# A slot table for a chunked recurrence: decay work three chunks ahead, the inverse spread over more slots, lower quarters of two batches one chunk later

## The chip, the cores and the metric

The kernel runs on one core of a Trainium2 chip. The metric is the device time of one execution in microseconds (us). TensorE (PE), VectorE (DVE), ScalarE (ACT), GpSimd (POOL) and SyncE (SP) run side by side, each works through its own instructions in order, and they wait for each other and for DMA transfers through semaphores.

## The reference

A linear recurrence with a rank-one correction is followed by a gated MLP and a top-1 mixture of experts. There are 4 batches, 8 heads, 768 tokens and 40 dimensions a head; the MLP is 320 to 1536 and back, and the mixture has 8 experts of 320 x 1024.

```python
for t in range(S):                                    # S = 768
    y[:, :, t] = einsum('bhd,bhde->bhe', rt, state)
    Sa = einsum('bhde,bhe->bhd', state, at)
    state = state * wt[:, :, None, :] - einsum('bhd,bhe->bhde', Sa, bt)
    state = state + einsum('bhd,bhe->bhde', vt, kt)
x = y as (B*S, H*D)                                   # 3072 x 320
x = ((x @ w_a) * (x @ w_b)) @ w_out
logits = x @ w_gate; e = argmax(logits)
out = softmax(logits)[e] * (relu(x @ w1[e]) @ w2[e])
```

## The kernel before, in words

The 768 tokens are cut into 12 chunks of 64. Within a chunk the recurrence becomes matrix products: the decays `w` are scanned into products from both sides, `a`, `b` and `k` are scaled by them, a 128 x 64 block of scores is made for each head, and a unit lower triangular 64 x 64 matrix is inverted for each batch and head. The inverse is made of two 32 x 32 diagonal blocks, done on VectorE for all heads at once in 31 steps of a multiply and a subtract (62 instructions, `tinv`), and of a lower quarter that joins them, done on TensorE (`t21a`, `t21b`).

`phase1` runs 13 passes of 24 slots, c = 0 to 12. In pass c stand beside each other:
- `A.stage`: the recurrence of chunk c itself, its state and outputs.
- `t21a` and `t21b` of the four batches b of chunk c+1. `t21a` transposes the upper diagonal block on VectorE into `t11`, and TensorE's product `ta` reads `t11`.
- The preparation of chunk c+2. `load` brings the decays `w` and `bk` (b and k together). `spans` is the check that all decays lie in the range for which the fast path is meant: four ACT activations, of which only the accumulated sums are kept and whose output `span` is thrown away. `scans` is a clip of `w`, a scan from behind (`suf`), a copy and a reciprocal, and a scan from ahead (into `w`). `scale_bk` is four VectorE multiplies of `bk` with `suf`. `scale_a` loads `at`, scales it on GpSimd and spreads it into the block-diagonal `ablk` by three DMAs. `scores` is TensorE's s1p from `bk` and `ablk`, ACT's copy, a mask on GpSimd, and after every second batch two DMAs into `nd` in DRAM. `rows` are transposes of `bk` into `kb`. `relayout` is a set of DMAs from `w` into `gp`. `tinv` starts with three DMAs, `m` in two halves from `nd` and `xt` from a constant, and ends with four DMAs into `td` in DRAM and four back into `s1`.
- MoE-up of chunk c-1: 24 groups of eight matmuls into a PSUM buffer `pm`, one in a slot from slot 2 on. ACT copies one group's result to `ua`, VectorE multiplies it with the next group's into `uh`, a slot later, and `hT<-uh` is sent two slots after that. `pm` has three buffers.
- Conversion of weights, and in passes 2 to 9 one DMA `xs<-zt` each, which fills an eighth of a table in DRAM with zeros (slot 17).

All other PSUM tiles of these stages come from five buffers `pa`. After the passes come the down projection, the gating and the experts.

TensorE, VectorE, ACT and GpSimd run in the order in which the program is written: the tables `STEADY` and `FIRST` (the latter for pass 0) give the slot of each piece. In a slot, the tasks that were put off with `dv.later(k, f)` are mixed evenly among the steps of the inverse; `ot.later(k, f)` are run at the head of the slot k later. SP, which issues nearly all DMAs, has an order of its own that a scheduler makes from the dependences. The completion semaphores of SP's DMAs are eight in rotation, and a DMA waits for the one that stands eight places ahead of it.

In the print below, `i` is the slot, `c1` and `c2` are the chunks one and two ahead.

Of the kernel before, what the change touches and what calls it, by code (L numbers as in the profile page):

```python
# [8 lines left out]
F32 = mybir.dt.float32  # L9
# [4 lines left out]
AF = mybir.ActivationFunctionType  # L14
# [118 lines left out]
def phase1(tc, I, cst, drm, psA, psM, ident, hT, mk_ident, wo, xs, span, tiny, down):  # L133
# [23 lines left out]
    mk_ident()  # L157
    A.zero([A.rblk])
    A.setup()
    A.spans(1)  # L160
    A.scale_a(0, 0)
    A.scale_a(0, 1)
    run(A.scale_bk(0))
# [35 lines left out]
    A.spans(0, [t[:120, 0:L // 2].bitcast(F32) for t in sp])  # L199
    units, tinv = [], []  # L200
    for c in range(NCH + 1):
        T = dict(STEADY)
        if c == 0:
            T.update(FIRST)
        assert T["span"] <= T["scan"] <= T["bk"] and T["scan"] < min(T["sa"])
        c1, c2 = c + 1, c + 2
        if c >= 1:
            units += M.groups(c - 1)
        if 0 < c < NCH:
            A.begin(c)  # L210
        at = lambda k, i: [b for b in range(B) if T[k][b] == i]
        for i in range(24):
            run(ot.take())
            if c == NCH and down:
                if i == LAST["free"]:
                    mid.close()
                    down.begin()
                    M.spare = down.p2
                if i >= LAST["gate"]:
                    run(down.gate_steps(1))  # L220
                for j in range(3):
                    if i == LAST["load"][j]:
                        down.load(j)
                for j in range(2):
                    if i == LAST["w"][j]:
                        down.load_w(4 * j + 4)
                    if i == LAST["conv"][j]:
                        down.conv(j)
            M.early = M.early and i < FIRST["early"]
            if c < NCH:  # L230
                A.stage(c, i)
            if c1 < NCH:
                for pr in range(2):
                    if i == T["vload"][pr]:
# [41 lines left out]
            n = min(len(tinv), T["steps"]) if i >= T["tinv"] else 0  # L276
            mix(tinv[:n], dv.take() + more)
            tinv = tinv[n:]
            if i == 23 and c2 < NCH:
                A.relayout(c2)  # L280
                tinv = A.tinv(c2)
            dv.now += 1
            ot.now += 1
# [7 lines left out]
    if not down:  # L291
# [76 lines left out]
class Attention:  # L368
    def __init__(self, tc, I, ctx1, ctx2, cst, drm, ps, ident, dv, ot, span):
# [64 lines left out]
    def spans(self, c, room=None):  # L434
# [65 lines left out]
    def scores(self, c, b):  # L500
# [9 lines left out]
        if b % 2 == 0:  # L510
# [1179 lines left out]
```

## Time and profile before

| | us |
|---|---|
| three runs | 1395.9, 1395.37, 1392.11 |
| their median | 1395.37 |
| the profiled execution | 1392.37 |
| its span in the trace | 1390.6 |
| passes 1 to 9 (175.7 to 856.0) | 680.3 |
| TensorE busy in its span | 1223.3 (88%) |
| VectorE, ACT, GpSimd busy | 682.6, 525.4, 428.1 |

The profile is one execution, recorded on the chip. A busy TensorE is one that has a matmul under way; the granted clock (PEclk) says at which of its levels, as a share of full speed, it ran over a stretch. The idle time of an engine is put down to what it waited for last. SPq is the issue of DMAs on SP. Passes of the slot loop are told apart by the first matmul of slot 0, `px<-sgT,at`.

### The profile page before, as it was taken

To read this page: it belongs to the slowest core of one execution; us is meant where nothing else is said; L and a number is where in the kernel's file an instruction comes from. 1 tells how busy PE (TensorE), PEld (TensorE's weight loads), DVE (VectorE), ACT (ScalarE), POOL (GpSimd) and SP (SyncE) were. 2 spreads that over 40 slices of the span, in tenths; PEclk is the share of its full clock that TensorE was granted. 3 is DMA by queue.
4 is the path that set the end of the run, shared out by engine and by line. 5 is a ranking of instruction groups with operands and counts; after the bars stand their busy time and mean duration, and the time that the engine had idled before them with its cause. 6 is when DMAs were issued, how large, how long until landed. Compare 5 with 4: busy or idle time off the path is not lost.

```text
span 1390.6 us, 27472 instructions
## 1 busy us (share of the span) xinstructions
PE 1223.3 (88%) x10474; PEld 1150.1 (83%) x10474; DVE 682.6 (49%) x1867; ACT 525.4 (38%) x1301; POOL 428.1 (31%) x488
## 2 busy tenths in 40 slices
PE   2306898989898999989898999999999989999995
PEld 2306798888897988888897889999999988999995
DVE  7487454452838265463737273611345676322321
ACT  3535532324343333434342423332333344444541
POOL 5443521111222213221222121213011254766650
PEclk9555569969898797999898999999899999999998
DMA  7353343435557364845443432313545554635420
GB/s 186 97 150 88 89 107 78 113 82 133 117 137 143 93 151 105 170 104 142 102 121 84 121 78 83 83 49 104 170 128 175 178 181 144 199 125 147 147 75 15
DMA packets 252909, 166.63 MB, mean 120 GB/s; under 512 B 158675, under 2 KB 236196, under 8 KB 252770
## 3 DMA queue, kind: packets, MB, share of 16 engines
q1 hardware_dynamic: 238545, 141.17, 40.0%
q0 software_dynamic: 9808, 15.76, 3.8%
q10 hardware_dynamic: 4416, 7.87, 2.0%
q8 instruction: 85, 1.39, 0.4%
q14 instruction: 55, 0.44, 0.1%
HBM read 111.76 MB, written 44.60 MB: 112 GB/s over the span
## 4 chain that ended last, share of the span: by engine, by line
PE 57%; DVE 18%; DMA 9%; issue 3%; ACT 3%; POOL 1%; SPq 1%; POOLq 0%; ACTq 0%; DVEq 0%
PE pm L929 14%; PE py L1066 7%; PE u L1355 6%; PE dn L1375 6%; DVE tmp L577 4%; DVE xt L583 4%; PE pu L700 3%; PE px L681 3%; PE ta L617 2%; DMA m<-nd 2%; PE py L762 2%; PE px L678 2%; PE s1p L506 2%; PE p L740 2%; PE pp L722 2%
## 5 line engine op out<-in xcount | busy, mean ns | idle before, releaser
L941 DVE TENSOR_TENSOR uh<-pm,ua 128x256 f32<-128x256 f32 x144 | 60.9, 423 | 307.1 <-PE pm L929 229.1
L929 PE MATMUL pm<-xl,wh 128*128 128x256 f32 x576 | 149.8, 344 | 30.8 <-DVE uh L941 30.3
L747 POOL TENSOR_SCALAR_AFFINE_SELECT s<-s 64x512 f32<-64x512 f32 x96 | 74.2, 773 | 257.8 <-ACT s L745 254.7
L577 DVE TENSOR_TENSOR tmp<-m,xt 128x126 f32<-128x126 f32 (+22 forms) x372 | 115.9, 314 | 28.7 <-DMA m<-nd 13.7
L929 PEld LDWEIGHTS pm<-xl,wh 128*128 128x128 f32 x576 | 94.9, 206 | 38.3 <-DVE uh L941 33.2
L929 PE MATMUL pm<-xh,wl 128*128 128x256 f32 x576 | 123.2, 298 | 0.0
L929 PE MATMUL pm<-xh,wh 128*128 128x256 f32 x576 | 122.4, 296 | 0.0
L583 DVE TENSOR_TENSOR xt<-xt,tmp 128x126 f32<-128x126 f32 (+22 forms) x372 | 116.0, 315 | 7.5
L932 ACT COPY ua<-pm 128x256 f32<-128x256 f32 x144 | 53.7, 373 | 163.1 <-PE pm L929 97.0
L1358 DVE SCALAR_TENSOR_TENSOR hl<-u,hh 128x384 fp32r<-128x384 f32 (+5 forms) x72 | 41.6, 581 | 140.9 <-ACT hh L1357 140.9
L929 PEld LDWEIGHTS pm<-xh,wl 128*128 128x128 f32 x576 | 96.7, 206 | 0.0
L929 PEld LDWEIGHTS pm<-xh,wh 128*128 128x128 f32 x576 | 96.7, 206 | 0.0
L1066 PE MATMUL py<-wh,hl 128*128 128x328 f32 x288 | 91.1, 316 | 2.2 <-DVE hl L1056 2.2
L1066 PE MATMUL py<-wl,hh 128*128 128x328 f32 x288 | 92.1, 320 | 0.6 <-DVE wl L1037 0.6
L908 POOL TENSOR_TENSOR xl<-xf,xh 128x192 fp32r<-128x192 f32 x48 | 29.0, 606 | 203.1 <-ACT xh L907 203.1
L1066 PE MATMUL py<-wh,hh 128*128 128x328 f32 x288 | 90.7, 315 | 0.0
L929 PE MATMUL pm<-xl,w 128*128 128x256 f32 x288 | 85.8, 298 | 0.0
L929 PE MATMUL pm<-xh,w 128*128 128x256 f32 x288 | 85.5, 297 | 0.0
L506 PE MATMUL s1p<-ablk,bk 120*128 120x192 f32 (+1 forms) x264 | 58.9, 378 | 28.6 <-DMA ablk<-at 21.7
L506 PEld LDWEIGHTS s1p<-ablk,bk 120*128 120x128 f32 x264 | 52.5, 234 | 30.7 <-issue 26.7
L681 PE MATMUL px<-vn,s 64*64 64x40 f32 x768 | 62.9, 246 | 15.4 <-ACT kb L534 15.4
L617 PE MATMUL ta<-t,s 32*32 32x32 f32 x768 | 34.2, 206 | 47.5 <-DVE t L614 46.4
(240 smaller groups left out, 3113.5 us busy)
## 6 DMA issues: line engine op xcount, KB each, us to landing
hT<-uh SPq DMA_DIRECT2D x72, 256.0 KB
hf<-hT SPq DMA_DIRECT2D x36, 512.0 KB
r<-in_moe_w SPq DMA_DIRECT2D x8, 1280.0 KB
r<-in_moe_w SPq DMA_DIRECT2D x8, 1024.0 KB
bk<-in_bk SPq DMA_DIRECT2D x11, 720.0 KB
xs<-zt SPq DMA_DIRECT2D x8, 805.0 KB
m<-nd SPq DMA_DIRECT2D x22, 256.0 KB
at<-in_a SPq DMA_DIRECT2D x24, 180.0 KB
```

Source lines behind the costliest of these rows:

```text
L506: nc.tensor.matmul(ps[:2 * C, 3 * g * C:(3 * g + n) * C], st["bk5"](b, g), self.ablk[b // 2][:, b % 2, g, 0:n, 0:C], start=True, stop=True)
L577: nc.vector.tensor_tensor(box[0], m[2 * s // R][:, s % (R // 2):s % (R // 2) + 1, s + 1:].to_broadcast([128, rows, n]), xt[:, :rows, s:s + ...
L583: nc.vector.tensor_tensor(xt[:, :rows, s + 1:], xt[:, :rows, s + 1:], box[0], op=ALU.subtract)
L617: nc.tensor.matmul(pa[R:C, R * h:R * h + R], s1[0:R, h, R:C], t11[:, h, :], start=True, stop=True)
L681: nc.tensor.matmul(px[:C, D * h:D * h + D], s1[C:2 * C, h, :C], vn[C:2 * C, D * h:D * h + D], start=(c == 0), stop=(c == 0 or h == H - 1))
L747: nc.gpsimd.affine_select(out=s2t[q * C:q * C + C], in_=s2t[q * C:q * C + C], pattern=[[0, 8], [1, C]], base=0, channel_multiplier=-1, com ...
L929: nc.tensor.matmul(p, l, r, start=(i == 0), stop=(i == len(seq) - 1))
L932: nc.scalar.copy(a, p)
L941: nc.vector.tensor_tensor(h[:, f % 2], p, a, op=ALU.mult)
L1066: self.nc.tensor.matmul(py, self.pair[i][l][:, k, s], self.W[r][:, first + k, cols], start=(first + k == 0 and n == 0), stop=(first + k == ...
L1355: nc.tensor.matmul(p, l, r, start=(i == 0), stop=(i == len(seq) - 1))
L1375: nc.tensor.matmul(p, l[:, q], r[:, f], start=(f == 0 and i == 0), stop=(f == len(hs) - 1 and i == 2))
```

## The change

The preparation is cut in two and put into other slots.
- `load` becomes `load_w` (slot 11, for chunk c+3) and `load_bk` (slot 0, for chunk c+2). `spans` and `scans` of chunk c+3 follow in slots 15, 16 and 16 to 21. Pass 0 does them twice, for chunk 2 in its first slots and for chunk 3 in its last.
- `spans` writes its throwaway output into an SBUF tile `junk`, not into PSUM.
- `scale_bk` goes to slots 2 and 3 (two multiplies each), `scale_a` to 2 and 5, the scores to 7, 8, 16, 17; `nd` is sent one slot after them.
- `relayout` goes to slot 10, `tinv` is begun in slot 22, and its 62 steps follow a list, in slots 2 to 16.
- `t21a` of batches 2 and 3 goes to slots 2 and 3 of the next pass, `t21b` to 5 and 6.

```diff
+            if 1 < c < NCH:
+                for b in at("t21a", i + 24):
+                    A.t21a(c, b)
+                for b in at("t21b", i + 24):
+                    A.t21b(c, b)
             if c2 < NCH:
...
                 if i == T["load"]:
-                    A.load(c2)
-                if i == T["span"]:
-                    A.spans(c2)
-                if i == T["scan"]:
-                    for f in A.scans(c2):
-                        dv.later(0, f)
-                if i == T["bk"]:
-                    for f in A.scale_bk(c2):
-                        dv.later(0, f)
+                    A.load_bk(c2)
+                for j, f in enumerate(A.scale_bk(c2) if i == T["bk"] else ()):
+                    dv.later(j // 2, f)
...
+                if i == T["relayout"]:
+                    A.relayout(c2)
+            if c3 < NCH:
+                if i == T["load_w"]:
+                    A.load_w(c3)
+                if i == T["span"]:
+                    for j, f in enumerate(A.spans(c3)):
+                        ot.later(1 + j // 2, f)
+                if i == T["scan"][0]:
+                    for j, f in zip(T["scan"], A.scans(c3)):
+                        dv.later(j - i, f)
...
-    "load": 0, "span": 3, "scan": 4, "bk": 6, "sa": [6, 10], "score": [10, 11, 18, 18],
-    "row": [11, 14, 23, 20], "t21a": [15, 15, 20, 20], "t21b": [20, 20, 23, 23], "steps": 8, "tinv": 3, "vload": [9, 20],
+    "load": 0, "bk": 2, "sa": [2, 5], "score": [7, 8, 16, 17], "row": [11, 14, 22, 23], "relayout": 10,
+    "load_w": 11, "span": 14, "scan": [16, 17, 20, 20, 21], "inverse": 22, "vload": [9, 20],
+    "t21a": [20, 20, 26, 27], "t21b": [22, 22, 29, 30],
+    "tinv": [0, 0, 2, 3, 5, 5, 2, 2, 5, 5, 5, 5, 5, 5, 5, 5, 3, 0, 0, 0, 0, 0, 0, 0],
...
-            junk = self.ps.tile([128, 6, C], F32, tag="pa", name=f"span{c}_{k}")
             nc.scalar.activation(
-                out=junk[:120], in_=wv[k // 2], func=AF.Relu,
+                out=self.junk, in_=wv[k // 2], func=AF.Relu,
```

In the listings below a number behind a name is that of the chunk (`m9` is the `m` of chunk 9), for `uh` and `pm` that of the MoE-up unit and group. The line numbers are each kernel's own.

VectorE in pass 8 before, slots 3 and 4, where decays of chunk 10 are scanned among steps of the inverse of chunk 9:

```order
L941 TENSOR_TENSOR uh7_0_8037<-pm7_0_1_8028,ua7_0_8007 128x256
L583 TENSOR_TENSOR xt9_7901<-xt9_7901,tmp9_4_8075 128x3x27
L462 TENSOR_SCALAR w10_7935<-w10_7935 120x12x64
L577 TENSOR_TENSOR tmp9_5_8080<-m9_7900,xt9_7901 128x78
L463 SCALAR_TENSOR_TENSOR suf10_8062<-w10_7935,d1_91 120x781
L583 TENSOR_TENSOR xt9_7901<-xt9_7901,tmp9_5_8080 128x3x26
L577 TENSOR_TENSOR tmp9_6_8084<-m9_7900,xt9_7901 128x100
L465 COPY gc10_8063<-suf10_8062 120x12
L583 TENSOR_TENSOR xt9_7901<-xt9_7901,tmp9_6_8084 128x4x25
L466 RECIPROCAL d1_91<-gc10_8063 120x12
L577 TENSOR_TENSOR tmp9_7_8089<-m9_7900,xt9_7901 128x96
L467 SCALAR_TENSOR_TENSOR w10_7935<-w10_7935,d1_91 120x780
```

The same engine in pass 8 now, slots 2 and 3:

```order
L976 TENSOR_TENSOR uh6_10_7832<-pm6_10_1_7823,ua6_10_7804 128x256
L649 STREAM_TRANSPOSE t11_8_2_7925<-s1_8_1_6653 32x256
L976 TENSOR_TENSOR uh6_10_7832<-pm6_11_1_7906,ua6_11_7876 128x256
L612 TENSOR_TENSOR tmp9_0_7956<-m9_7807,xt9_7808 128x31
L525 TENSOR_TENSOR bk10_7864<-bk10_7864,suf10_7575 120x6x64
L618 TENSOR_TENSOR xt9_7808<-xt9_7808,tmp9_0_7956 128x31
L525 TENSOR_TENSOR bk10_7864<-bk10_7864,suf10_7575 120x6x64
L649 STREAM_TRANSPOSE t11_8_3_7971<-s1_8_1_6653 32x256
L612 TENSOR_TENSOR tmp9_1_7994<-m9_7807,xt9_7808 128x30
L525 TENSOR_TENSOR bk10_7864<-bk10_7864,suf10_7575 120x6x64
L618 TENSOR_TENSOR xt9_7808<-xt9_7808,tmp9_1_7994 128x30
L525 TENSOR_TENSOR bk10_7864<-bk10_7864,suf10_7575 120x6x64
```

The scans are gone from there, the multiplies of `bk10` stand where the inverse begins, and `t11` of chunk 8's last batch, which stood in the pass before, follows the second of them.

SP before, around the end of pass 7, from the DMAs of chunk 9's `nd` to the load of chunk 10's `bk`:

```order
L667 DMA uv8_0_7913<-in_vt 120x3x64
L521 DMA nd9_7024<-s1_9_1_7678 32x16x32 x2
L659 DMA rblk_95<-in_r 40x6x64
L568 DMA m9_7900<-nd9_7024 64x1x1024 x2
L659 DMA rblk_95<-in_r 40x6x64 x2
L943 DMA hT_67<-uh6_8_7721 128x2x256
L664 DMA r8_0_7911<-in_r 120x192
L427 DMA bk10_7937<-in_bk 120x1536
```

SP now, at the same place:

```order
L550 DMA nd9_6955<-s1_9_1_7571 32x16x32 x2
L978 DMA hT_67<-uh6_6_7536 128x2x256
L677 DMA vn_98<-in_vn 64x2x320
L603 DMA m9_7807<-nd9_6955 64x1x1024 x2
L606 DMA xt9_7808<-in_one 128x512
L978 DMA hT_67<-uh6_8_7674 128x2x256
L694 DMA rblk_96<-in_r 40x6x64 x3
L699 DMA r8_0_7840<-in_r 120x192
L702 DMA uv8_0_7842<-in_vt 120x3x64
L455 DMA bk10_7864<-in_bk 120x1536
```

Between the second half of `m9` and `bk10` stand now seven DMAs, among them `xt9`; the two `gp` of the relayout, which stood ahead of `m` in most passes, are gone to slot 10.

SP now in pass 4, where the inverse of chunk 5 ends:

```order
L505 DMA at7_1_5307<-in_a 120x384
L290 DMA xs_72<-zt_109 128x10x161 x2
L629 DMA td0_1_105<-xt5_4144 512x1x32 x2
L629 DMA td1_1_106<-xt5_4144 512x1x32 x2
L633 DMA s1_5_0_3546<-td0_1_105 32x16x32
L633 DMA s1_5_1_3907<-td0_1_105 32x16x32
L634 DMA s1_5_0_3546<-td1_1_106 32x16x64
L634 DMA s1_5_1_3907<-td1_1_106 32x16x64
L550 DMA nd6_4202<-s1_6_1_4820 32x16x32 x2
```

Two of the zero-fills stand right ahead of the transfers of the inverse; before, the nearest one stood behind the loads of the next pass.

## Rows read from the trace of the kernel before

**Rows 1.** Passes 1, 4, 9, 10; sum of passes 2 to 9. Columns: us, busy (records), PEclk.

```profile
175.70:252.50 76.80, 72.48 (x665) 66.78 (x664) 37.56 (x107) 28.29 (x78) 14.58 (x22) 0.83 0.38 94
...
408.90:490.80 81.90, 76.31 (x682) 70.66 (x681) 40.66 (x113) 28.55 (x80) 18.55 (x26) 0.81 0.57 125
...
785.00:856.00 71.00, 66.30 (x681) 61.36 (x680) 37.06 (x103) 24.76 (x68) 13.56 (x19) 0.95 0.41 100
856.00:914.30 58.30, 58.30 (x646) 54.01 (x645) 29.23 (x94) 19.05 (x52) 8.70 (x13) 1.00 0.30 76
...
sum 603.50, PE 560.27 PEld 518.64 DVE 321.29 ACT 216.99 POOL 139.14; mean PE 70.03 PEld 64.83 DVE 40.16 ACT 27.12 POOL 17.39
```

**Rows 2.** The page's costliest groups: scores and lower quarters; busy, mean ns, idle before.

```profile
L506 PE MATMUL s1p<-ablk,bk 120*128 120x192 f32 (+1 forms) x264 | 58.9, 378 | 28.6 <-DMA ablk<-at 21.7
...
L617 PE MATMUL ta<-t,s 32*32 32x32 f32 x768 | 34.2, 206 | 47.5 <-DVE t L614 46.4
```

**Rows 3.** Waits of TensorE in passes 1 to 9: us in total, times, longest.

```profile
PE pm L929 <- DVE uh L941: 30.3, 16, 3.2
PE px L678 <- ACT s L514: 5.7, 3, 2.3
PE pp L722 <- ACT span L445: 5.7, 3, 2.3
```

**Rows 4.** VectorE's timeline in pass 9: start, length, instruction, idle before.

```profile
795.88 0.42 DVE L941 TENSOR_TENSOR uh<-pm,ua 128x256 f32<-128x256 f32 x1 [1.90 <-PE pm L929]
...
799.32 0.56 DVE L462 TENSOR_SCALAR w<-w 120x768 f32<-120x768 f32 x1 [2.87 <-ACT span L445]
...
799.98 1.78 DVE L463 TENSOR_TENSOR_SCAN suf<-w,d 120x781 f32<-120x781 f32 x1
...
812.33 0.42 DVE L941 TENSOR_TENSOR uh<-pm,ua 128x256 f32<-128x256 f32 x1
```

**Rows 5.** VectorE's groups by line in pass 9: busy us, mean ns, idle.

```profile
L583 DVE TENSOR_TENSOR xt<-xt,tmp 128x126 f32<-128x126 f32 (+22 forms) x31 | 9.3, 300 | 0.7
...
L496 DVE TENSOR_TENSOR bk<-bk,suf 120x384 f32<-120x384 f32 x4 | 2.2, 553 | 0.0
...
L614 DVE STREAM_TRANSPOSE t<-s 32x256 f32<-32x256 f32 x4 | 1.5, 410 | 2.1 <-DMA s<-td 2.1
```

**Rows 6.** DMA issues on SP in pass 4: start, length, what, times.

```profile
412.79 0.34 SPq L427 DMA_DIRECT2D bk<-in_bk  x1
...
417.35 3.41 SPq L273 DMA_DIRECT2D xs<-zt  x2
...
429.04 4.07 SPq L486 DMA_DIRECT2D ablk<-at  x3
434.99 0.38 SPq L943 DMA_DIRECT2D hT<-uh  x1
```

**Rows 7.** DMA issues on SP from pass 8 into pass 9.

```profile
771.71 3.48 SPq L547 DMA_DIRECT2D gp<-w  x4
775.29 1.18 SPq L568 DMA_DIRECT2D m<-nd  x2
...
781.29 0.38 SPq L943 DMA_DIRECT2D hT<-uh  x1
...
789.84 0.47 SPq L421 DMA_DIRECT2D w<-in_w  x1
```

**Rows 8.** Waits of SP's issues from 770 to 802 us.

```profile
SPq L421 <- DMA m<-nd: 1.7, 1, 1.7
```

**Rows 9.** Waits of SP's issues from 409 to 440 us.

```profile
SPq L273 <- DMA bk<-in_bk: 2.1, 1, 2.1
...
SPq L943 <- DMA xs<-zt: 1.0, 1, 1.0
```

**Rows 10.** TensorE's timeline at the start of pass 8.

```profile
712.76 0.77 PE L678 MATMUL px<-sgT,at 120*64 120x120 f32 x6
...
722.33 0.50 PE L929 MATMUL pm<-xl,wh 128*128 128x256 f32 x2
```

More of the change, by code (lines that the diff above doesn't have):

```diff
@@ L159, in phase1 @@
     A.setup()
-    A.spans(1)
+    run(A.spans(1))
     A.scale_a(0, 0)
@@ L198, in phase1 @@
     mix(both, [lambda b=b: A.stage0(0, b) for b in range(2)] + conv.take(FIRST["conv1"][1]))
-    A.spans(0, [t[:120, 0:L // 2].bitcast(F32) for t in sp])
+    run(A.spans(0, [t[:120, 0:L // 2].bitcast(F32) for t in sp]))
     units, tinv = [], []
@@ L204, in phase1 @@
             T.update(FIRST)
-        assert T["span"] <= T["scan"] <= T["bk"] and T["scan"] < min(T["sa"])
-        c1, c2 = c + 1, c + 2
+        c1, c2, c3 = c + 1, c + 2, c + 3
         if c >= 1:
@@ L243, in phase1 @@
                     A.t21b(c1, b)
-            if c2 < NCH:
-                if i == T["load"]:
-                    A.load(c2)
-                if i == T["span"]:
-                    A.spans(c2)
-                if i == T["scan"]:
-                    for f in A.scans(c2):
-                        dv.later(0, f)
-                if i == T["bk"]:
-                    for f in A.scale_bk(c2):
-                        dv.later(0, f)
+            if 1 < c < NCH:
[3 more added lines that the diff above has]
+                    A.t21b(c, b)
+            if c2 < NCH:
+                if c == 0:
+                    if i == 0:
+                        A.load_w(c2)
+                        for f in A.spans(c2):
+                            f()
+                    if i == 1:
+                        for f in A.scans(c2):
+                            dv.later(0, f)
+                if i == T["load"]:
+                    A.load_bk(c2)
+                for j, f in enumerate(A.scale_bk(c2) if i == T["bk"] else ()):
+                    dv.later(j // 2, f)
                 for pr in range(2):
@@ L275, in phase1 @@
                     zt[:, None, :].to_broadcast([128, 2 * nz // XW, XW // 2]))
-            n = min(len(tinv), T["steps"]) if i >= T["tinv"] else 0
+            n = T["tinv"][i]
             mix(tinv[:n], dv.take() + more)
             tinv = tinv[n:]
-            if i == 23 and c2 < NCH:
-                A.relayout(c2)
+            if i == T["inverse"] and c2 < NCH:
+                assert not tinv
                 tinv = A.tinv(c2)
@@ L322 @@
         2, 2, 2, 4, 1, 1, 3, 0, 3, 0, 1, 1],
-    "conv0": [20, 5, 10, 16], "conv1": [10, 30], "lead": 5, "early": 12, "steps": 1, "load": 0,
-    "span": 0, "scan": 1, "bk": 5, "sa": [3, 5], "score": [9, 12, 13, 15], "row": [12, 13, 23, 23],
-    "t21a": [8, 9, 14, 15], "t21b": [9, 12, 18, 16],
+    "conv0": [20, 5, 10, 16], "conv1": [10, 30], "lead": 5, "early": 12, "load": 0, "bk": 5, "sa": [3, 5], "score": [9, 12, 13, 15], "row": [12, 13, 23, 23],
+    "t21a": [8, 9, 14, 15], "t21b": [9, 12, 18, 16], "tinv": [0] * 24, "relayout": 17, "load_w": 18,
+    "span": 19, "scan": [21, 21, 22, 22, 23],
 }
@@ L380, in __init__ @@
         self.d1 = p1.tile([120, L], F32, name="d1")
+        self.junk = p1.tile([120, 6, C], F32, name="junk")
         ms(self.d1, 0.0)
@@ L416, in load, with load_w, load_bk @@
     def load(self, c, room=None):
-        nc = self.nc
+        w, bk = room if room else (None, None)
+        self.load_w(c, w)
+        self.load_bk(c, bk)
+    def load_w(self, c, room=None):
         st = self.st[c] = {"s1": {}, "kb": {}, "at": {}}
-        st["w"], bk = room if room else (self.p1.tile([120, L], F32, tag="w", name=f"w{c}"), None)
-        nc.sync.dma_start(st["w"], self.src("w", "w", c))
-        if room:
+        st["w"] = self.p1.tile([120, L], F32, tag="w", name=f"w{c}") if room is None else room
+        self.nc.sync.dma_start(st["w"], self.src("w", "w", c))
+    def load_bk(self, c, bk=None):
+        nc, st = self.nc, self.st[c]
+        if bk:
             for h in range(2):
@@ L442, in spans, with one @@
         wv = [cut(x) for x in w]
-        for k in range(4):
-            junk = self.ps.tile([128, 6, C], F32, tag="pa", name=f"span{c}_{k}")
+        def one(k):
             nc.scalar.activation(
-                out=junk[:120], in_=wv[k // 2], func=AF.Relu,
+                out=self.junk, in_=wv[k // 2], func=AF.Relu,
                 scale=1.0 if k % 2 else -1.0, bias=self.wlim[:, k % 2:k % 2 + 1], accum_out=self.span[:, k, c:c + 1])
+        return [lambda k=k: one(k) for k in range(4)]
     def scans(self, c):
@@ L517, in scores, with send @@
             channel_multiplier=-1, compare_op=ALU.is_gt, fill=0.0)
-        if b % 2:
+        def send():
             for k in range(2):
@@ L523, in scores @@
                     s1p[q, :, :, q].rearrange("p b h t -> p (b h) t"))
+        if b % 2:
+            if c < 2:
+                send()
+            else:
+                self.ot.later(1, send)
     def rows(self, c, b):
```

## The prediction

> **What bounds the kernel now.** The first view to read is busy time by stretch, one stretch for each pass of the slot loop [rows 1]. Pass 10 lasts 58.3 us and TensorE is busy for all of it at clock 1.00: with the same inverse (62 VectorE steps, 8 in a slot) but no preparation of a chunk behind it, TensorE is the only bound. Pass 9 does 36 matmul records more (682 against 646), those of four scores and four rows, and lasts 71.0 us: 4.7 us idle and clock 0.95. At pass 10's 58.3/646 = 0.09 us a record the 36 would add 3.2 us; at the scores' 58.9/264 = 0.22 us for their 24 and 0.09 for the other 12 they would add 6.4 [rows 2]. I take 4.7, near the middle, so an undisturbed pass is 63.0 us. The eight passes 2 to 9 last 603.5 us, hence 603.5 - 504.0 = **99.5 us lost**, of which 603.5 - 560.3 = 43.2 us are idle; the rest is matmuls at the lower of TensorE's two granted levels (1.2 GHz beside 2.4) after the gaps. Lost time per idle microsecond is 2.3 over all, 8.0/4.7 = 1.7 in pass 9, 18.9/5.6 = 3.4 in pass 4. So a gap costs about twice its length, and a forecast of this change is one of gaps.
>
> The second view is TensorE's waits over passes 1 to 9 [rows 3]: 30.3 us in 16 gaps of at most 3.2 us where MoE-up waits for VectorE's `uh`, which frees a PSUM buffer of three; 5.7 us for the ACT copy of the scores; 5.7 us for the range check, whose throwaway output takes four of five PSUM buffers `pa`. The third view, VectorE's timeline in pass 9, says why [rows 4]: two `uh` stand 16.4 us apart. Between them VectorE waits 2.87 us for the range check, does the clip and two scans of one length (0.56 + 2 x 1.78 = 4.1 us, with two short instructions between them some 4.5) and two slots of eight inverse steps. All that is in one slot of about 2.6 us.
>
> **The change part by part.** Per chunk every engine keeps its work, so nothing is to be had from busy times; only waits move.
>
> Decays three chunks ahead, scans in slots 16 to 21, `scale_bk` in slots 2 and 3 instead of 6: slot 4 loses 4.5 us and the 2.87 us wait. The inverse goes from eight steps a slot (slots 3 to 10) to two to five (slots 2 to 16). A step is a multiply and a subtract, counted singly, of 0.30 us [rows 5], so a slot holds at most 1.5 us of them; beside the `uh` of 0.4 and some instructions of about 0.5 that is up to 4 us once, else under 3, beside 2.6 us of TensorE. The 30.3 us go nearly whole. Pass 10 shows that the steps alone cost TensorE nothing. The scans of 1.78 us now stand among slots 16 to 21, where VectorE has no inverse; each can hold up a `uh` by at most its length, and three PSUM buffers give two slots: nothing, at most 1.8 us a pass.
>
> The range check into SBUF frees `pa`: the 5.7 us [rows 3] go, and the four activations keep their cost on ACT, now two in a slot; as ACT is busy for 24.8 of 71.0 us [rows 1], bound 0 to 1 us a pass, I take 0. Scores in slots 7, 8 and 16, 17 with nd sent a slot later: the 5.7 us for the copy go. The spread of `a` (three DMAs) is due at slot 7 instead of 10. By the order it stands behind `bk` and gp on SP; at 429.04 SP issued three in 4.07 us [rows 6], so with bk at the time worked out below, and a landing as long as bk's own behind it, it is there by about +17 us of the pass, and slot 7 asks at about 7/24 of 63 = +18: nothing, 0 to 3 us.
>
> The lower quarters of batches 2 and 3 move to slots 2 and 3 of the next pass. Their TensorE work (0.71 us a batch, 34.2 us for 48 batches [rows 2]) moves one pass on and costs nothing by itself. But **a new wait comes with it**. In the new order VectorE does t11 of batch 3 behind the first two of the four `bk` multiplies, so behind the arrival of `bk`; and TensorE stands in order behind t11. When is `bk` there? SP's DMAs use eight completion semaphores in turn, so each waits for the one eight places ahead: in [rows 7, 8] w, eighth behind the second half of m, waited 1.7 us for m<-nd; in [rows 6, 9] hT, eighth behind the second zero-fill xs, waited for xs. In the new order `bk` is the one eighth behind m's second half. Working it out in microseconds from the start of a pass:
> m's issue before: the second half's at 776.47 - 0.59 = 775.9 [rows 7], and pass 9 starts at 785.0, so -9.1. The gp issues ahead of it (3.48 us) leave for slot 10: -12.6; an hT and a vn come in ahead (0.4 us each, by hT's row in [rows 7]): -11.8.
> m lands 789.84 - 775.9 = 13.9 us after its issue [rows 7, 8]: +2.1. bk's own issue 0.4: +2.5.
> bk lands: issued at 412.79, and the second xs, eighth behind it, waited 2.1 us for it and ended its issue at 420.76, so 6.7 to 8.0 us; I take 7.2 [rows 6, 9]: +9.7.
> Then 0.55 + 0.30 + 0.55 us for two multiplies and one step, and 0.41 for t11 [rows 5]: +11.5. With a few tenths for starts on SP and VectorE: +12.0.
> TensorE asks for t11 of batch 3 in slot 3 behind its 16 pu matmuls. In pass 8 those end 722.33 - 712.76 = 9.6 us after the start (the 722.33 row follows them) [rows 10]; with batch 2's 0.7 us of quarters ahead, less overlap, at +10.0.
> So TensorE waits **2.0 us** a pass, bounds 0.4 (the lower landing, and the 0.7 us in full) to 7 (bk's landing stretched as far as the zero-fill stretches others). Passes 2 to 9 have it; pass 1 hasn't (chunk 1's quarters are done in pass 0), nor 10 and 11 (no bk).
>
> The zero-fills of `xs` make it longer in five passes. In the new order those of chunks 3 to 6 stand right ahead of the inverse's td transfers, and one in pass 2 between s and nd. Such a fill of 805 KB lands about 15 us after its issue (420.0, and hT waited until 434.99 [rows 6, 9]). Eighth behind the second fill is the last of the s transfers, and nd and m stand behind that. The fill is issued when SP, running ahead, comes to it: between slot 13 and slot 16 (+35 to +42 of 63), so it lands at +50 to +57, and m, due at 63.0 - 11.8 = +51.2, goes out 0 to 8 us late. I take 3.7: those passes wait 5.7 us at t11, in the pass after each fill.
>
> Sum of new waits: 3 x 2.0 + 5 x 5.7 = 34.5 us in passes 2 to 9. Times 1.8 for the clock (pass 9's 1.7, since these too are one gap a pass, and a little more for the five longer ones): 62.1 us lost instead of 99.5, **37.4 saved**. Pass 1 (76.8 us with 4.3 idle) loses its range-check and `uh` waits: 5 us, 2 to 10. Pass 0 gets a second set of range check and scans with TensorE waiting for other things there: 0 to 5 us lost, I take 0. Prologue, passes 10 to 12 and the expert stage keep their instructions. Sum: 1392.4 - 42.4 = 1350.0 us against the profiled execution. That one lies 2.1 us under the mean of the three runs and 3.0 under their median, so I predict **1352**.
>
> **The rivals.** (B) *`bk` comes in time.* For it: only 2 us are missing, and m's 13.9 us were measured beside hT and rblk traffic that also moves. Against: 13.9 us for two 256 KB halves is long where zero-fills of 805 KB take 15, so it looks like the transfer's own shape. The Trainium skill, "DMA: Bandwidth & Descriptors", section "Why a DMA increments its semaphore by 16 and not by 1", says that a DMA is split over the largest number of engines up to 16 that divides the slowest dimension of both sides; m's source has a slowest dimension of 2. By that rule m keeps its time whatever the traffic, which the row allows. With gaps of 0.4 us left: 8 x 0.4 x 1.8 = 6 lost, 1392.4 - 99.5 - 5 + 6 + 2 = 1296.
>
> (C) *Slower: the m to bk chain lengthens itself.* A late t11 delays stage 1 of batches 2 and 3, they delay scores and nd, and so the next m. From a mean wait of (99.5 + 5)/(8 x 1.8) = 7.3 us a pass it eats all the gain, that is, when bk lands later than about +15. For it: bounds of the fills above reach 8 us more. Against: after the wait the pass has 50 us in which nothing depends on it. At 8.0 us: 115 lost, 1405.
>
> (D) *The gaps at `pm` stay.* The 30.3 us would then be too few PSUM buffers, not VectorE's queue. What speaks against is pass 10, no idle with the same three. If they stay, 30.3 x 2.3 = 70 us stay, and the waits for t11 of 2.0 us add 29: 1389. The Trainium skill names this one: "Perfetto Trace Analysis", section "Optimization Strategy", takes the same gap repeating on the engine that should be saturated as a sign of too few buffers; here [rows 4] show one late reader instead.
>
> (E) *The clock falls for longer.* One gap of 2 to 6 us early in a pass may cost like pass 4 (3.4) rather than pass 9 (1.7). At 2.85, between the two and the mean: 34.5 x 2.85 = 98, only 1.2 and the 5 us are saved: 1388.
>
> **How the numbers follow.** Forecast 0.54, B 0.14, C 0.13, D 0.09, E 0.10. 0.3% (about what a measurement can tell from no change) is 4.2 us: faster is below 1391.2. Faster: 0.54 + 0.14 + half of D and E, 0.06 and 0.05, = 0.79; same 0.08 (the rest of D and E), slower 0.13. The forecast's own range, waits of 1 to 3 us and fills of 2 to 6 more at 1.7 to 2.3, is 1322 to 1380. The range for 8 in 10 leaves out C and the lower part of B: 1300 to 1392.
>
> **What would show it.** Right: no `uh` wait over 1 us left on TensorE in passes 2 to 9; one gap a pass at ta behind t11, ten to twelve us after its start, with VectorE's bk multiply just before and the DMA bk<-in_bk as its releaser; SP waiting for m ahead of bk; range-check and score-copy waits gone; passes of about 66.6 us, in the five after fills about 73. Wrong: gaps at pm (D); no gap at ta and passes near 63 (B); gaps over 7 us, growing from pass to pass (C); gaps as forecast but the granted clock under 0.85 (E); or a wait at a place not named, such as slot 7 for `ablk` or slot 20 for s<-td.

## The result and the profile after

The changed kernel takes **1350.43 us** (median of four runs, 1346.84 to 1353.26) against 1393.74 us before (1389.49 to 1395.9): ratio 0.969, 95% interval 0.966 to 0.973. Some runs come out slower at a lower granted clock; every ratio here leaves such runs out. The profiled execution has a span of 1348.2 us, 42.4 less than before. The forecast was 1352.

The first view is again busy time by stretch: passes 2 to 9 together, pass 1 and pass 10 of the changed kernel (columns as in [rows 1]).

```profile
251.04:811.78 560.74, 530.53 (x5442) 490.80 (x5441) 311.74 (x879) 218.99 (x596) 153.90 (x197) 0.95 0.54 125
177.35:251.04 73.69, 67.27 (x602) 62.05 (x601) 44.68 (x110) 30.25 (x82) 15.71 (x22) 0.83 0.41 101
811.78:870.87 59.09, 59.09 (x646) 54.44 (x645) 29.79 (x94) 19.27 (x52) 8.80 (x13) 1.00 0.27 68
```

Passes 2 to 9 fell from 603.5 to 560.7 us: 42.8 us, all of the gain. Their idle time went from 43.2 to 560.74 - 530.53 = 30.2 us, and the matmuls themselves take 29.7 us less at the same count, since the granted clock rose from 0.89 (the same stretch before) to 0.95. Pass 1 gained 3.1 us, though its idle time rose from 4.3 to 6.4: it has 63 matmul records fewer (602, before 665 [rows 1]), as quarters of two batches went on to pass 2. Pass 1 starts 1.7 us later than before (177.35, before 175.70), and all that follows pass 9 takes 1.8 us longer.

What TensorE waits for in passes 2 to 9, and then in pass 1 (us in total, times, longest):

```profile
PE ta L652 <- DVE t L649: 15.9, 4, 9.3
PE ta L652 <- DVE tmp L612: 7.9, 4, 3.5
PE p L775 <- ACT uv L750: 5.8, 2, 4.4
PE py L797 <- POOL s L782: 0.7, 2, 0.4
...
PE sgp L725 <- DVE xf L814: 6.4, 1, 6.4
```

The three lines of [rows 3] are gone: no wait for `uh`, for the range check or for the copy of the scores. In their place stands `ta` behind `t`, the lower quarters behind t11, 23.8 us. Seven of its eight gaps lie in slot 3 (20.8 us); one of 2.95 us, in slot 20 of pass 4, is for the inverse's own transfer.

The 5.8 us at `p` are one gap of 1.4 us in pass 3 and one of 4.4 in pass 5. In pass 5 ACT, which copies `uv`, first stands at a conversion of weights that waits for a DMA:

```profile
527.83 0.40 ACT L372 CAST wo<-c_f 128x256 fp32r<-128x256 f32 x1 [7.58 <-DMA wo<-wo]
528.14 0.31 ACT L750 COPY uv<-pv 120x192 f32<-120x192 f32 x1
```

The 6.4 us of pass 1 are again a reader behind decays just loaded, now by pass 0's second set: ACT waits 5.6 us for them, VectorE 3.9 us for ACT's range check, and `xf` follows the scan.

```profile
184.21 0.56 DVE L491 TENSOR_SCALAR w<-w 120x768 f32<-120x768 f32 x1 [3.90 <-ACT junk L472]
```

Pass 8, which starts at 678.97, shows the chain step by step. First SP's issues there, and what the load of `bk` waited for:

```profile
668.08 1.20 SPq L603 DMA_DIRECT2D m<-nd  x2
...
683.58 0.48 SPq L455 DMA_DIRECT2D bk<-in_bk  x1
...
SPq L455 <- DMA m<-nd: 1.8, 1, 1.8
```

Then VectorE and TensorE:

```profile
689.88 0.56 DVE L525 TENSOR_TENSOR bk<-bk,suf 120x384 f32<-120x384 f32 x1 [3.89 <-DMA bk<-in_bk]
690.35 0.18 DVE L618 TENSOR_TENSOR xt<-xt,tmp 128x31 f32<-128x31 f32 x1
690.45 0.55 DVE L525 TENSOR_TENSOR bk<-bk,suf 120x384 f32<-120x384 f32 x1
690.92 0.42 DVE L649 STREAM_TRANSPOSE t<-s 32x256 f32<-32x256 f32 x1
```

```profile
688.10 1.12 PE L735 MATMUL pu<-xs,s 64*64 64x40 f32 x16
691.49 1.03 PE L652 MATMUL ta<-t,s 32*32 32x32 f32 x16 [2.27 <-DVE tmp L612]
```

`bk` is issued when m has landed, 4.6 us into the pass; SP waits for m ahead of `bk` in all eight passes, 12.5 us in total. The first two multiplies start at +10.9, t11 ends at +12.4, and TensorE, done with pu at +10.2, waits 2.27 us. The forecast had +2.1 for the landing of m, then +9.7, +12.0, +10.0 and 2.0. The name `tmp` in the wait is a neighbour: the instruction on VectorE that began nearest to the release. The `bk` line with its 3.89 us says what it was.

### The profile page after: what moved, and what is told of

Read it like the earlier page. It is cut to its first block, busy times and chain, and to the rows that moved or that the text cites. A ratio compares the mean times of both kernels' runs of the same rounds, so it can differ in the third digit from the quotient of the medians.

```text
span 1348.2 us, 27424 instructions
## 1 busy us (share of the span) xinstructions
PE 1192.2 (88%) x10474; PEld 1120.2 (83%) x10474; DVE 679.9 (50%) x1867; ACT 531.7 (39%) x1301; POOL 444.0 (33%) x488
## 4 chain that ended last, share of the span: by engine, by line
PE 66%; DMA 15%; DVE 7%; issue 4%; POOL 3%; ACT 3%; SPq 1%; POOLq 0%; DVEq 0%; ACTq 0%
PE pm L964 19%; PE py L1101 8%; PE dn L1410 5%; PE u L1390 5%; DMA hT<-uh 4%; PE py L797 3%; PE px L716 3%; PE s1p L535 3%; PE p L775 3%; DMA at<-in_a 3%; PE pp L757 2%; PE py L793 2%; PE pu L735 2%; PE px L713 2%; PE ta L652 2%
## 5 line engine op out<-in xcount | busy, mean ns | idle before, releaser
L964 PE MATMUL pm<-xl,wh 128*128 128x256 f32 x576 | 144.5, 333 | 0.5 <-POOL xl L943 0.5
L964 PE MATMUL pm<-xh,wl 128*128 128x256 f32 x576 | 118.8, 289 | 0.0
L964 PE MATMUL pm<-xh,wh 128*128 128x256 f32 x576 | 118.0, 287 | 0.0
L618 DVE TENSOR_TENSOR xt<-xt,tmp 128x126 f32<-128x126 f32 (+22 forms) x372 | 111.0, 302 | 7.6
L964 PEld LDWEIGHTS pm<-xl,wh 128*128 128x128 f32 x576 | 90.3, 197 | 6.3 <-POOL xl L943 0.7
L964 PEld LDWEIGHTS pm<-xh,wh 128*128 128x128 f32 x576 | 92.4, 197 | 0.0
L964 PEld LDWEIGHTS pm<-xh,wl 128*128 128x128 f32 x576 | 92.3, 196 | 0.0
L652 PEld LDWEIGHTS ta<-t,s 32*32 32x32 f32 x768 | 30.7, 117 | 71.5 <-ACT junk L472 41.4
L535 PE MATMUL s1p<-ablk,bk 120*128 120x192 f32 (+1 forms) x264 | 54.2, 350 | 26.0 <-DMA ablk<-at 21.6
L1410 PE MATMUL dn<-l,hh 128*128 128x320 f32 (+3 forms) x240 | 74.9, 312 | 0.0
```

The source lines that it names most:

```text
L535: nc.tensor.matmul(ps[:2 * C, 3 * g * C:(3 * g + n) * C], st["bk5"](b, g), self.ablk[b // 2][:, b % 2, g, 0:n, 0:C], start=True, stop=True)
L618: nc.vector.tensor_tensor(xt[:, :rows, s + 1:], xt[:, :rows, s + 1:], box[0], op=ALU.subtract)
L652: nc.tensor.matmul(pa[R:C, R * h:R * h + R], s1[0:R, h, R:C], t11[:, h, :], start=True, stop=True)
L964: nc.tensor.matmul(p, l, r, start=(i == 0), stop=(i == len(seq) - 1))
L1410: nc.tensor.matmul(p, l[:, q], r[:, f], start=(f == 0 and i == 0), stop=(f == len(hs) - 1 and i == 2))
```

## The experiments

Each kernel ran beside the kernel before on the same chip. On these chips the runs of the kernel before that enter the ratios spread over 1376 to 1398 us, more than in the first comparison, so the ratios have wide intervals, and times from different chips are compared by their ratios; what is said of causes rests on the profiles. All diffs but that of the three `b` kernels are against the changed kernel.

### e1_bk5: bk multiplied after the quarters

```diff
-    "load": 0, "bk": 2, "sa"
+    "load": 0, "bk": 5, "sa"
```

> The changed kernel with the four bk multiplies in slots 5 and 6 instead of 2 and 3, so that t11 of batch 3 stands ahead of them on VectorE; all else as changed (1350.4 us). Theory (TensorE's waits at ta in slot 3 are the arrival of bk and nothing else; 20.8 us in passes 2 to 9 at 1.9 us lost per us idle): the waits at ta behind bk go, some 3 us stay in pass 3, where bk lands 18 us after the start and the scores of slot 7 want it; about 1317 us, 1310 to 1328. Rival (the wait moves: uh or the scores stand behind the same multiplies and TensorE waits there instead): gaps of the same sum at pm or s1p, 1342 to 1352 us.

1327.2 us (1323.8 to 1327.6), ratio 0.957 [0.946, 0.968], where the changed kernel had 0.969. TensorE's waits from pass 1 on:

```profile
PE sgp L725 <- DVE xf L814: 6.1, 1, 6.1
PE ta L652 <- DVE t L649: 5.4, 2, 3.1
PE s1p L535 <- ACT s L780: 3.1, 4, 0.8
PE ta L652 <- DVE tmp L612: 2.6, 1, 2.6
...
sum 540.49, PE 525.50 PEld 485.61 DVE 311.99 ACT 219.92 POOL 146.50; mean PE 65.69 PEld 60.70 DVE 39.00 ACT 27.49 POOL 18.31
```

The slot-3 gaps are gone but for 2.6 us in pass 3, and passes 2 to 9 (the sum) take 540.5 instead of 560.7 us. The two gaps of 5.4 us are slot 20's. The scores of slot 7 now wait 0.7 to 0.8 us in six passes, but not as the rival has it: in pass 8 VectorE is through with `bk` 2.7 us before they begin. They begin 4.2 us after SP starts to issue `ablk`, as in e4_quarters below, where the profile names `ablk`. So the order of t11 behind `bk` is the cause of most of the gaps in slot 3, and worth 20 us in this profile, some 17 by the two ratios.

### e8_bk_act: bk not behind m

```diff
-            nc.sync.dma_start(t, self.src("bk", "bk", c))
+            (nc.scalar if c >= 3 else nc.sync).dma_start(t, self.src("bk", "bk", c))
```

> The changed kernel with the load of bk (from chunk 3 on) issued from ScalarE's queue instead of SP's, at the same slot 0, so that it doesn't stand eighth behind the second half of m. Theory (bk is late because SP holds its issue back until m has landed): bk is issued within 1 to 2 us of the pass's start and lands by +10, the waits at ta in slot 3 fall under 1 us in most passes, 1315 to 1332 us. Rival (bk lands late because the DMA engines are busy with rblk, r and m then): it is issued earlier and lands no earlier, ta waits stay near 20 us, 1343 to 1355 us.

1337.6 us (1335.2 to 1344.2), ratio 0.963 [0.957, 0.970]: between the two. ScalarE issues `bk` 2.3 or 2.4 us into each of passes 2 to 9, where SP in the changed kernel did so between +1.1 (pass 5) and +11.8 (pass 3). In six of them VectorE waits for `bk`, and of these pass 6 (from 526.64) has the longest travel; VectorE has `bk` at +10.1, 7.8 us after its issue:

```profile
528.96 0.33 ACTq L455 DMA_DIRECT2D bk<-in_bk  x1
...
536.77 0.56 DVE L525 TENSOR_TENSOR bk<-bk,suf 120x384 f32<-120x384 f32 x1 [2.35 <-DMA bk<-in_bk]
```

Over the six it takes 5.9 to 7.8 us; in the changed kernel it took 5.8 to 6.7 (6.3 in pass 8). So SP did hold `bk` back, but a `bk` issued earlier mostly travels longer, and little is won: outside pass 3 the gaps at ta sum to 8.1 us, where the changed kernel has 11.5. As a way to remove the wait the theory fails. Of the idle time of passes 2 to 9, 10.8 us less than in the changed kernel, half was won in slot 3 (15.5 us there, before 20.8) and half elsewhere, the wait in slot 20 of pass 4 among it, which is gone here too. Nor is the edit a clean one: once in each pass SP now waits for `bk` itself, 2.2 to 12.8 us, before it goes on to `rblk`, `r` or `uv`. Pass 3 kept 7.4:

```profile
331.95 0.19 DVE L612 TENSOR_TENSOR tmp<-m,xt 128x31 f32<-128x31 f32 x1 [9.01 <-DMA r<-in_r]
332.06 0.55 DVE L525 TENSOR_TENSOR bk<-bk,suf 120x384 f32<-120x384 f32 x1
```

There `bk` is ready as soon as its turn comes, and the inverse's first step ahead of it waits. That step reads m, which went out 3 us ahead of the pass (10 ahead of pass 2), since nd, behind a zero-fill, held it for 4.3 us. (The `r` in the row is a neighbour; SP, which sent m out at 312.6 to 313.8, waits 1.2 us for it until 331.29.) So in pass 3 the late piece is m itself.

### e5_fill_out: zero-fills elsewhere

```diff
-            if 2 <= c < 10 and i == T["fill"]:
-                if c == 2:
+            if c in (10, 11) and i in (3, 8, 13, 18):
+                if c == 10 and i == 3:
                     A.zero([zt])
-                k = nz * (c - 2)
+                k = nz * (4 * (c - 10) + i // 5)
```

> The changed kernel with the eight zero-fills xs moved out of passes 2 to 9 into passes 10 and 11 (four each), where no chunk is prepared. Theory, from the trace of the changed kernel (m is issued 12 us ahead of the next pass in pass 4 too, fills or not; the fills cost the 3 us wait for s<-td in slot 20 of pass 4 and some of pass 3's 9.3 us): ta waits of 2 to 3 us stay in slot 3, 1335 to 1350 us. Rival, the prediction's step (the fills delay m and so bk by some 4 us in five passes): slot 3's waits at ta fall to 2 us everywhere and the passes 3 to 7 lose 18 us of idle, 1315 to 1330 us.

1344.9 us (1334.5 to 1346.5), ratio 0.964 [0.957, 0.972]: as the theory from the trace had it. The gaps in slot 3 of passes 2 to 9 sum to 20.2 us, where the changed kernel has 20.8; pass 3's fell from 9.3 to 3.9, pass 5's came up from none to 4.6. In pass 3 the second half of m goes out at -7.7 instead of -2.5 (the fill did hold it up), in pass 5 at -7.4 instead of -11.8. Without any fill m starts out 8.0 to 8.4 us ahead of passes 3, 5 and 7 (gaps of 3.7 to 4.6) and 10.4 to 11.0 ahead of the others (0.6 to 2.6); why every second one is late stays open.

The wait in slot 20 of pass 4 is gone, and so are those at `p` for `uv`: ACT waits 1.3 us for `wo` in passes 2 to 9, where the changed kernel has 15.0. These passes last 550.7 us, 10.0 less. So the fills did cost time there, but, pass 3 apart, not by way of m. Pass 10, to which four fills went, shows this:

```profile
801.35:867.15 65.80, 64.36 (x645) 59.16 (x644) 29.94 (x94) 19.31 (x52) 8.98 (x14) 0.91 0.70 130
```

One gap of 1.4 us, clock 0.91, and the pass is 6.7 us longer than the 59.1 of the changed kernel.

### e4_quarters: the lower quarters in their own pass

```diff
-    "t21a": [20, 20, 26, 27], "t21b": [22, 22, 29, 30],
+    "t21a": [20, 20, 21, 21], "t21b": [22, 22, 23, 23],
```

> The changed kernel with the lower quarters of batches 2 and 3 in their own pass again (t21a in slot 21, t21b in 23), so that nothing of TensorE's slots 2 and 3 stands behind bk but uh. Theory (t11 behind bk is the cause; uh behind the same wait has two slots of slack by the three PSUM buffers): the ta waits of slot 3 go; bk that is over 6 us behind its slot shows at pm instead (pass 3 some 5 us, else 0 to 2), and slot 21 waits up to 1 us a pass for s<-td: 1318 to 1338 us. Rival (whatever stands behind bk on VectorE waits as long): 20 us of gaps at pm in passes 2 to 9, 1348 us or more.

1338.6 us (1334.9 to 1346.9), ratio 0.966 [0.955, 0.977]. The waits from pass 1 on:

```profile
PE s1p L535 <- DMA ablk<-at: 16.8, 7, 3.6
PE sgp L725 <- DVE xf L814: 6.4, 1, 6.4
PE ta L652 <- DVE t L649: 6.2, 2, 4.1
```

The slot-3 gaps are gone and nothing waits at pm, which is what the theory says; the rival's gaps at pm didn't come. But `ablk`, the spread of `a` for slot 7, now arrives 1.4 to 3.6 us late in seven passes, and passes 2 to 9 last 559.2 us in the profiled run (the slowest of the five), hardly less than in the changed kernel. That isn't only because the gap of slot 3 closed: e1_bk5 has none there in most passes either and waits 0.8 us at most. Here the quarters are gone from ahead of slot 7 as well, so that TensorE asks for its scores 2.8 us earlier (in pass 8 at +17.7, in e1_bk5 at +20.5).

### e3_steps8: the old pace of the inverse

```diff
-    "tinv": [0, 0, 2, 3, 5, 5, 2, 2, 5, 5, 5, 5, 5, 5, 5, 5, 3, 0, 0, 0, 0, 0, 0, 0],
+    "tinv": [0, 0, 0, 8, 8, 8, 8, 8, 8, 8, 6, 0, 0, 0, 0, 0, 0, 0, 0, 0, 0, 0, 0, 0],
```

> The changed kernel with the inverse again at eight steps a slot from slot 3 (slots 3 to 10), all else as changed. Theory (the uh waits of the kernel before came from the decay scans and their wait for the range check in slot 4; the steps by themselves cost TensorE nothing, as pass 10 showed): at most 0.5 us a pass more idle, 1348 to 1360 us. Rival (the list is what removed the 30 us of uh waits): uh waits of 15 us or more in passes 2 to 9 come back, 1375 us or more.

1340.6 us (1339.7 to 1345.1), ratio 0.967 [0.956, 0.978], no worse than the changed kernel and under the theory's 1348. No wait for `uh` came back:

```profile
PE ta L652 <- DVE t L649: 20.0, 7, 7.8
PE sgp L725 <- DVE xf L814: 6.4, 1, 6.4
PE s1p L535 <- ACT uv L750: 3.3, 3, 2.2
```

The list of steps is not what brought the gain.

### e6_scan_in_inverse: the scans among eight steps

```diff
-    "tinv": [0, 0, 2, 3, 5, 5, 2, 2, 5, 5, 5, 5, 5, 5, 5, 5, 3, 0, 0, 0, 0, 0, 0, 0],
+    "tinv": [0, 0, 0, 0, 0, 8, 8, 8, 8, 8, 8, 8, 6, 0, 0, 0, 0, 0, 0, 0, 0, 0, 0, 0],
-    "relayout": 10, "load_w": 11, "span": 14, "scan": [16, 17, 20, 20, 21]
+    "relayout": 6, "load_w": 6, "span": 9, "scan": [11, 11, 11, 11, 11]
```

> The kernel e3_steps8 (eight steps a slot, 1340.6 us) with the relayout and the load of the decays in slot 6, the range check in slots 10 and 11 and all five scan instructions in slot 11, among eight steps of the inverse (now slots 5 to 12). The range check doesn't wait there for decays just loaded. Theory (the uh waits of the kernel before came from scans that stand in one slot with eight steps of the inverse): some 7 us of VectorE work in slot 11 beside 2.6 us of TensorE, so a uh wait of 1 to 3 us in most passes: 10 to 20 us of waits at pm, 1360 to 1380 us. Rival (they came from the wait for the range check, not from the work): no uh wait over 0.5 us, 1335 to 1350 us.

1335.3 us, a single run. The rival was right:

```profile
PE ta L652 <- DVE t L649: 9.8, 5, 7.5
PE pv L749 <- ACT vn L737: 6.8, 3, 3.1
PE sgp L725 <- DVE xf L814: 6.2, 1, 6.2
PE kbp L566 <- ACT s L666: 2.9, 2, 1.6
```

No `uh` wait at all, with 4.5 us of scans among eight steps in one slot. At the clip VectorE waits 0.2 us in passes 2 to 9 here; in the kernel before it was 15.7 us:

```profile
L491 DVE TENSOR_SCALAR w<-w 120x768 f32<-120x768 f32 x7 | 3.9, 558 | 0.2 <-issue 0.2
```

```profile
L462 DVE TENSOR_SCALAR w<-w 120x768 f32<-120x768 f32 x8 | 4.5, 561 | 15.7 <-ACT span L445 12.3 <-DMA uv<-in_vt 3.4
```

This points at the wait, not the work; the next three kernels take it to the kernel before.

### b1_junk, b2_scan7, b3_both: parts alone on the kernel before

b1_junk has only the range check's output in SBUF. b2_scan7 has only later slots for the check and what follows it; b3_both has both.

```diff
-    "load": 0, "span": 3, "scan": 4, "bk": 6, "sa": [6, 10], "score": [10, 11, 18, 18],
-    "row": [11, 14, 23, 20],
+    "load": 0, "span": 5, "scan": 7, "bk": 8, "sa": [8, 10], "score": [12, 13, 18, 18],
+    "row": [13, 15, 23, 20],
```

> The kernel before with one part of the change alone: the range check's output goes into SBUF, everything stays in its slot. Theory (the three waits of 5.7 us in all at pp came from the four buffers pa; the uh waits of 30.3 us come from VectorE's wait for the same check, which stays): the waits at pp go, the uh waits stay at 25 to 33 us; 6 us of idle less at 1.9, about 1382 us, 1376 to 1390. Rival (PSUM held nothing up that ACT's wait for the decays doesn't hold up anyway): 1390 to 1395 us.

> The kernel before with only these tasks later in the pass: range check slot 5 instead of 3, scans 7 instead of 4, bk 8 instead of 6, a 8 instead of 6, scores 12, 13 instead of 10, 11, rows 13, 15 instead of 11, 14. The decays are still loaded in slot 0 of the same pass, the scans still stand in one slot with eight steps of the inverse. Theory (from e6_scan_in_inverse: the uh waits are VectorE standing behind a check that stands behind decays just loaded, and not the amount of VectorE's work): VectorE's wait at the clip, 15.7 us in passes 2 to 9, goes, and the uh waits fall from 30.3 to under 8 us; 1335 to 1362 us. Rival (4.5 us of scans beside eight steps in one slot are the cause): uh waits of 20 us or more stay, 1378 us or more.

> The two edits b1_junk and b2_scan7 together on the kernel before. Theory: with both gone what is left is the copy of the scores and the inverse's s<-td, 10 to 15 us idle in passes 1 to 9; 1325 to 1352 us, at most 10 us below b2_scan7. Rival (they remove the same wait, so nothing is added): within 4 us of the faster of the two.

b1_junk: 1378.8 us (1369.9 to 1383.9), ratio 0.9945 [0.990, 0.999]. b2_scan7: 1357.8 us (1352.2 to 1363.8), ratio 0.984 [0.979, 0.990]. b3_both: 1352.0 us (1350.2 to 1353.1), ratio 0.979 [0.974, 0.983]. The line for `uh` in each, in this order (30.3 before):

```profile
PE pm L929 <- DVE uh L941: 37.7, 17, 3.2
```

```profile
PE pm L929 <- DVE uh L941: 16.7, 8, 3.0
```

```profile
PE pm L929 <- DVE uh L941: 17.0, 9, 2.5
```

b1_junk's wait at pp is gone, but the `uh` waits took up as much as it left (37.7 for 30.3); its ratio is 0.9945 where 0.992 was expected, inside the interval. In b2_scan7 the check comes two slots later and the scans three; VectorE's wait at the clip falls from 15.7 to 0.0 us in passes 2 to 9, and the `uh` waits to about half. Neither theory is whole: about half of the 30 us was the wait for decays just loaded, and some 17 us stay, one gap in each of passes 2 to 9 at +28 or so. In pass 8 the two `uh` around it stand 8.9 us apart, and VectorE has no idle time between them: it does the scans, steps of the inverse and three products of the recurrence. That this work is the cause of the remainder is argued, not shown; in e6_scan_in_inverse scans among eight steps cost nothing. Small waits appear elsewhere in b2_scan7 (8.4 us at px for `xf`). b3_both has two thirds of the whole change's gain (2.1 of 3.1%).

### e2_span_psum: the range check in PSUM again

```diff
-                out=self.junk, in_=wv[k // 2], func=AF.Relu,
+                out=self.ps.tile([128, 6, C], F32, tag="pa", name=f"span{c}_{k}")[:120], in_=wv[k // 2], func=AF.Relu,
```

> The changed kernel with the range check's throwaway output in PSUM again (four of the buffers pa), in its new slots 15 and 16. Theory (it cost 5.7 us of TensorE idle in passes 1 to 9 before because ACT stood at it waiting for the decays just loaded; in the new slots the decays are long there and each buffer is held for about 1 us): 0 to 0.5 us a pass, 1350 to 1357 us. Rival (four of five buffers taken at once hold TensorE up wherever they stand): the 5.7 us come back at the clock's factor of 1.9, about 1361 us, with waits behind the activations in slots 15 to 17.

1354.2 us (1352.7 to 1355.0), ratio 0.977 [0.966, 0.988]. In the theory's range. Behind the check itself stand 0.9 and 0.2 us in all of passes 1 to 9, and one gap of 6.3 us at the end of pass 0, where the decays have just been loaded; the changed kernel's 6.4 us at sgp in pass 1 are gone in return:

```profile
PE pz L809 <- ACT span L472: 6.3, 1, 6.3
PE pv L749 <- ACT span L472: 0.9, 1, 0.9
...
PE pp L757 <- ACT span L472: 0.2, 1, 0.2
```

### e7_combo: a better version

`bk` as in e1_bk5, fills as in e5_fill_out, and in pass 0:

```diff
-    "tinv": [0] * 24, "relayout": 17, "load_w": 18,
+    "tinv": [0] * 24, "relayout": 9, "load_w": 10,
```

> The changed kernel with bk multiplied in slots 5 and 6 (as e1_bk5, 1327 us), the zero-fills in passes 10 and 11 and, in pass 0, the relayout and the next load of decays at slots 9 and 10 instead of 17 and 18. Theory: of the 21 us idle that e1_bk5 has left in passes 1 to 9, the 5.4 at slot 20 go with the fills, pass 3's 2.6 mostly, and pass 1's 6.1 at sgp with the earlier decays; at 2 us lost per us idle 1297 to 1312 us. Rival (other waits take their place, the lost clock stays): 1318 to 1328 us.

1309.7 us (1304.6 to 1320.8), ratio 0.944 [0.937, 0.951]; better than both kernels. Pass 4 has no idle left, and passes 2 to 9 (the sum) have 4.8 us; then pass 10 with four fills, which has a gap of 1.7 us:

```profile
377.87:441.55 63.68, 63.68 (x682) 59.03 (x681) 39.08 (x113) 29.02 (x80) 20.03 (x26) 1.00 0.55 131
...
sum 515.70, PE 510.92 PEld 472.74 DVE 314.84 ACT 220.82 POOL 148.63; mean PE 63.86 PEld 59.09 DVE 39.35 ACT 27.60 POOL 18.58
...
764.05:824.86 60.81, 59.13 (x646) 54.44 (x645) 29.75 (x94) 19.22 (x52) 9.04 (x14) 1.00 0.73 136
```

Pass 1 kept 4.3 of 6.1 us at sgp: with the earlier decays in pass 0 about a third of it went. What holds the rest wasn't tried.

## Why the prediction was right, and where it was not

**The sum.** Forecast for passes 2 to 9: 504 + 62.1 = 566.1 us; measured 560.7. The undisturbed pass, taken as 63.0, is 63.68 in e7_combo. Idle time 34.5 forecast, 30.2 measured. Lost per idle us 1.8 forecast; (560.7 - 504)/30.2 = 1.9. Pass 1: 5 us forecast from waits that go; they went, but the wait behind pass 0's second set took their place, and the 3.1 us measured come with the quarters that moved on. Pass 0: nothing taken of 0 to 5, 1.7 lost up to the start of pass 1. That the total is right within 2 us is partly luck: errors offset each other.

**The new wait** was right in place, cause and size: t11 behind `bk` behind m, 2.0 us forecast, 1.8 and 2.3 in passes 2 and 8, 0.4 in pass 9. Its working had m's issue at -11.8 and landing at +2.1; they were -10.3 and +4.6, with `bk`'s travel 6.3 instead of 7.2 us. e1_bk5 shows that t11's place behind `bk` makes the wait. That m's hold makes `bk` late is shown for its issue alone: without the hold it landed little earlier (e8_bk_act). m itself took 13 to 15 us from issue to landing in all eight passes, as forecast, but not whatever the traffic: in pass 3 of e8_bk_act, with `bk` under way beside it, 18.

**The zero-fills** are the step that failed. Forecast: 5.7 us in passes 3 to 7. Measured: 9.3, 2.8, none, 0.9, 3.5, together 16.5. And without fills in those passes they sum to 15.4 (e5_fill_out). The argument was that the last s transfer waits for the fill's landing. In the trace of the changed kernel two fills are issued at 440.7 in pass 4, yet m goes out at 460.7 to 462.2, some 12 us ahead of pass 5 at 473.5: on time. The fills went out at +45, later than the forecast's +35 to +42, and yet no issue of SP in passes 2 to 9 waits for a fill. A fill held m up in one place, ahead of pass 3, where it stood between s and nd; what the fills cost besides was 2.95 us in slot 20 for s<-td, which the forecast didn't price, and 5.8 us at `p` for `uv`, named nowhere in it; both went with the fills. So 5 x 3.7 = 18.5 of the 34.5 us were priced by a wrong mechanism. The five passes came out near their forecast all the same (72.1 us on average, about 73 forecast), which is luck.

**The uh waits** went whole, as forecast, but the forecast took [rows 4] as one sum, the 2.87 us idle at the clip, 4.5 us of scans and sixteen steps, and didn't say what each is worth. In b2_scan7 the wait at the clip goes and half of the `uh` waits with it. e6_scan_in_inverse has the scans among eight steps a slot, away from the load, and no `uh` wait; e3_steps8 has the old pace of the steps and none either, so the part given to the step list isn't confirmed.

**The range check**: its price of 0 to 1 us a pass in the new slots is right: in passes 2 to 9 TensorE waits nowhere for it. But the 5.7 us didn't need SBUF to go: with the output in PSUM and the check in its new slots they stay away as well (e2_span_psum). **ablk**: nothing taken, 0 to 3 bounded; it is nothing in the changed kernel, also in passes 5, 6 and 9, where slot 3's gap is under 1 us, and 1.4 to 3.6 us where slot 7 comes sooner (e4_quarters).

**The rivals.** B (1296): `bk` didn't come in time, but passes 6 and 9 at 64.56 and 64.11 us come near it, and e7_combo, where nothing early in the pass waits for `bk`, has passes of 63.7 to 64.8. C: no growth from pass to pass; the waits after pass 3 are smaller. D: pm has no wait for `uh`; the three buffers were enough. The Trainium skill ("Perfetto Trace Analysis", section "Optimization Strategy") says that the same gap repeating can mean too few buffers; here 30.3 us of such gaps went with the same three. E: the clock was 0.95, not under 0.85. In the chances, half of D's 0.09 is 0.045, not 0.06; nothing hangs on it.

## What to carry to other kernels

Idle time on the bounding engine that repeats with each pass can be another engine standing in order behind a transfer just issued; here moving the reader some slots later was worth more than thinning out the work around it. When a piece is moved across a pass, look at what stands ahead of it in its engine's new place, and how late that can arrive: here putting a 0.4 us transpose ahead of the multiplies instead of behind two of them gave about 20 us. Where gaps close, later slots come sooner and can find a transfer not yet there (`ablk` in e4_quarters), so price edits one after the other.

## What the runs showed of the hardware

The price of a gap in clock is not fixed. In pass 10, one gap of 1.4 us in slot 20 (e5_fill_out) came with a clock of 0.91 and 6.7 us lost; one of 1.7 us in the same place (e7_combo) with 1.00 and 1.7 us lost. In both kernels the matmuls are the same; what stood ahead differs: passes 2 to 9 had 20.2 us idle at a clock of 0.93 to 0.97 there, and 4.8 us at 1.00 here. Which of it decides wasn't tried.

A transfer issued earlier didn't arrive earlier by as much: from SP's issue, 1.1 to 11.8 us into the pass, `bk` took 5.8 to 6.7 us until VectorE used it, from ScalarE's at +2.3 it took 5.9 to 7.8. That it travels beside m then is likely (m took 18 us in pass 3 there, 13 to 15 in the changed kernel), but wasn't tried apart.
